# Down-projection: six sums of seven paired and woven matmul by matmul, with three weight forms moved to other tiles

## The chip, the cores and the metric

The kernel runs on one core of one Trainium2 chip. The metric is the device time of one execution in microseconds (us), the median of several runs. Below, PE is TensorE (matmuls), PEld its weight loads, DVE is VectorE, ACT is ScalarE, POOL is GpSimd, and SP is SyncE, which issues most DMAs. Inside the profiled execution, times are counted from the first instruction of the program.

## The reference, cut to what matters

```python
g = sigmoid((x * gate_w).sum(-1, keepdims=True))      # x: (2, 1, 4096, 640)
a = A_ref(x, w1, b1, w2, b2)      # real FFT, complex block MLP, soft threshold, inverse FFT
b = (gelu(x @ w_gate) * (x @ w_up)) @ w_down          # 640 -> 1728 -> 640
return g * a + (1 - g) * b
```

The change lies in the last product, the down-projection `h @ w_down`: 8192 tokens, 1728 rows of weights, 640 columns of output.

## The kernel before, in words

**Precision.** All operands are fp32 numbers split in two: a high part that ACT rounds (`high`, line 275) and a low part, the rest, that DVE subtracts (`low`, line 278). A product is three matmuls: high by high, low by high, high by low. `split` makes both parts.

**Order of the work.** First the gate and up projections (line 472, `run`, with 256 columns to a matmul), interleaved with the forward transform; then the spectral MLP; last, from about 1810 us on, the down-projection with the last stage of the inverse transform. This last stage is a loop of 32 steps over `c_seq` (batch and a pair of token groups of 128 tokens each).

**One step of the down-projection.** Two token groups are multiplied together by Winograd's scheme for 2 by 2 blocks: seven products instead of eight. Each product multiplies a combination of the hidden activations (`a11`, `s2`, `s3`, `s1`, `a12`, `a22`, `s4`) by a combination of the weights (`b11`, `t2`, `t3`, `t1`, `b21`, `t4`, `b22`, called forms). A product sums over seven chunks `j` of 128 rows into one PSUM bank: 21 matmuls of 128 by 128 by 320 columns, and 20 where the last chunk is half empty (the forms in `HALF`). That is 144 matmuls a step. In each, the activations are the stationary operand (`ho`) and the weights (`wx`) the moving one: for each `j`, high activations with high weights, low with high, high with low. In front of these, `inv2` (line 1161) does 12 matmuls of the inverse transform.

`down` (line 1188) does the seven products one after another, in the order of the list above, each followed by DVE or ACT work that reads the bank. Between two products stands a hook. The hooks call `step(k)` (line 1459), in which the operands of later products are made: `h_load` (DMA of four activation tiles for the next step), `h_s3`, `h_s2`, `h_s1` (sums on POOL), `h_s4` (on DVE), `h_op` (the split of one activation operand: two ACT and two or three DVE instructions), `c_load` and `c_split` (the inverse transform's data: two DMAs, then four splits), `v_load` (its matrix, issued by POOL), and `flush` (the stores that were put aside). Each engine executes its instructions in the order in which the code emits them; waits are made from the dependences.

**Tiles.** SBUF tiles come from tags with a fixed number of buffers: `big` (18 of 5120 bytes to a partition), `small` (18 of 2560), `tiny` (15 of 1024), `mid` (14 of 4096). The first three start at multiples of 128 bytes. Between them and `mid` lies a spacer of 112 words, 448 bytes, which is three and a half times 128, so each `mid` tile starts 64 bytes past a multiple of 128. Below, a tile or slice that starts at a multiple of 128 bytes is called plain and one that starts 64 bytes past it shifted. 1280 bytes, the width of one form's part, is ten times 128, so neighbouring parts in one tile are alike. In `c_split` (line 1105) the high parts start 16 words into a `mid` tile, which makes them plain, and the low parts 32 or 352 words, which leaves them shifted. A buffer that is reused waits for the last use of what it held; of the free ones, the one that has been free longest is taken. The weights stay in 14 `big`, 6 `small` and 10 `mid` tiles for the whole stage, so four `big` buffers are left for activation operands, and one operand takes one.

**Which part of a form lies where.** The parts are written to DRAM (`wdf`, `wdl`) by `wd_pre` in columns that `HI` and `LO` (lines 1011 and 1012) number, and read back by `wd_load`: columns 0 to 7 into two `big` tiles, 8 and 9 into a `small` one, 10 to 12 into a `mid` tile, and the one part in `wdl` into a `mid` tile for three `j`. So before the change the high parts of all seven forms, and the low parts of `b11`, `t2`, `t3`, are plain; the low parts of `t1` (from `wdl`), `b21`, `b22`, `t4` are shifted.

**The loads of the weights** are spread by hand over the last steps of the spectral MLP (the table `fin`, line 1412). Those of `S + 1`, the last, and of hook 0 of the first down step stand together in the SP queue.

Of the kernel before, what the change touches and what calls it, by code (L numbers as in the profile page):

```python
# [15 lines left out]
P = 128  # L16
# [197 lines left out]
def spectral_mix_kernel(ctx: ExitStack, tc: tile.TileContext, a):  # L214
# [793 lines left out]


    FORMS = ["b11", "t2", "t3", "t1", "b21", "t4", "b22"]  # L1010
    HI = {"b11": 0, "t2": 2, "b21": 4, "t3": 5, "t1": 6, "t4": 8, "b22": 9}
    LO = {"b11": 1, "t2": 3, "t3": 7, "b21": 10, "b22": 11, "t4": 12}

    def wd_pre(j):
        o = {}
        pair = (j, j + 6) if j < 6 else (12, 13)

        def loads():
            for t in pair:
                wd_raw(t)  # L1020

        def sums(k):
            def f():
                if not o:
                    r1, r2 = (RAW.pop(("d", t)) for t in pair)
                    o.update(b11=r1[:, :320], b12=r1[:, 320:], b21=r2[:, :320], b22=r2[:, 320:])
                n, p, q = (("t1", "b12", "b11"), ("t2", "b22", "t1"), ("t3", "b22", "b12"), ("t4", "b21", "t2"))[k]
                if k % 2 == 0:
                    o["x"] = small([P, 2, 320], name="wx")
                o[n] = o["x"][:, k % 2]  # L1030
                nc.vector.tensor_sub(o[n], o[p], o[q])
            return f

        def form(n):
            def f():
                w = small([P, 2, 320], F32R, name="wf")
                if j == 6 and n in HALF:
                    x = o[n][:64]
                    nc.gpsimd.memset(w[64:, 1].bitcast(F32), 0.0)
                    split(w[:64, 0], w[:64, 1], x)  # L1040
                    high(w[64:, 0], x)
                else:
                    split(w[:, 0], w[:, 1], o[n])
                if n == "t1":
                    st(dr(wdf[j], 320 * HI[n], [[13 * 320, P], [1, 320]]), w[:, 0].bitcast(F32))
                    st(dr(wdl, 320 * j, [[7 * 320, P], [1, 320]]), w[:, 1].bitcast(F32))
                else:
                    st(dr(wdf[j], 320 * HI[n], [[13 * 320, P], [320 * (LO[n] - HI[n]), 2], [1, 320]]), w.bitcast(F32))
# [11 lines left out]
    def wd_load(j, part):  # L1060
# [9 lines left out]
        if part < 2:  # L1070
            t = big([P, 4, 320], F32R, name="wx")
            go(t.rearrange("p h d -> p (h d)"), wdf[j], 13, 4 * part, 4)
            for k, (n, h) in enumerate((("b11", 0), ("b11", 1), ("t2", 0), ("t2", 1)) if part == 0 else
                                       (("b21", 0), ("t3", 0), ("t1", 0), ("t3", 1))):
                put(n, h, t[:, k])
        elif part == 2:
            if j < 6:
                t = small([P, 2, 320], F32R, name="wx")
                go(t.rearrange("p h d -> p (h d)"), wdf[j], 13, 8, 2)
                put("t4", 0, t[:, 0])  # L1080
# [3 lines left out]
            for k, n in ((0, "b21"), (352, "b22"), (672, "t4")):  # L1084
                put(n, 1, x[:, k:k + 320])
        else:
            x = mid([P, 1024], F32R, name="wx")
            n = 3 if j < 6 else 1
            go(x[:, :320 * n], wdl, 7, j, n)
            for k in range(n):  # L1090
                WM.setdefault(j + k, {}).setdefault("t1", [None, None])[1] = x[:, 320 * k:320 * k + 320]
            if j == 6:
                go(x[:, 336:976], wdf[6], 13, 8, 2)
                put("t4", 0, x[:, 336:656])
                put("b22", 0, x[:, 656:976])

    def c_load(i):
# [90 lines left out]
    def down(i, u, hooks):  # L1188
# [4 lines left out]
        c1, c2 = slice(0, 320), slice(320, 640)  # L1193
        acc = lambda: bank()[:, :320]

        def blk(a_, b_):
            h = HO.pop((i, a_))
            ops = []
            for j, (hh, hl) in enumerate(h):
                wh, wl = WM[j][b_]  # L1200
                ops += [(hh, wh), (hh, wl)] if j == 6 and a_ in HALF else [(hh, wh), (hl, wh), (hh, wl)]
            return ops
        hooks[0]()
        e = small([P, 2, 320], name="e")
        A = acc()
        run(A, blk("a11", "b11"))
        nc.scalar.activation(e[:, 0], A, AF.Copy)
        hooks[1]()
        B = acc()
        run(B, blk("s2", "t2"))  # L1210
        nc.vector.tensor_add(e[:, 0], B, e[:, 0])
        hooks[2]()
        C = acc()
        run(C, blk("s3", "t3"))
        nc.vector.tensor_add(e[:, 1], C, e[:, 0])
        hooks[3]()
        E = acc()
        run(E, blk("s1", "t1"))
        for x in (E, e[:, 1]):
            nc.vector.scalar_tensor_tensor(u2[:, c2], x, g2, u2[:, c2], op0=OP.mult, op1=OP.add)  # L1220
        hooks[4]()
        run(A, blk("a12", "b21"), first=False)
        nc.vector.scalar_tensor_tensor(u1[:, c1], A, g1, u1[:, c1], op0=OP.mult, op1=OP.add)
        hooks[5]()
        Dd = acc()
        run(Dd, blk("a22", "t4"))
        nc.vector.tensor_add(e[:, 1], Dd, e[:, 1])
        nc.vector.scalar_tensor_tensor(u2[:, c1], e[:, 1], g2, u2[:, c1], op0=OP.mult, op1=OP.add)
# [4 lines left out]
        nc.vector.scalar_tensor_tensor(u1[:, c2], e[:, 0], g1, u1[:, c2], op0=OP.mult, op1=OP.add)  # L1233
        st(out[b, n1], u1)

# [172 lines left out]
    def events(i, j):  # L1408
        for f, *args in todo.get((i, j), []):
# [11 lines left out]
           S - 2: [(h_load, 0, 0), *wl(1, 2), (h_load, 0, 1)],  # L1421
           S - 1: [(c_split, 0), (h_op, 0, "a11"), *wl(1, 3, 4, 5), *wl(0, 6), (h_s3, 0, nc.gpsimd), (c_load, 1)],
           S: [(h_s2, 0), (h_op, 0, "s2"), (c_split, 1)],
           S + 1: [*wl(1, 6), *wl(3, 0, 3, 6), (flush,), *wl(2, 6), (wd_later,), *wl(2, 4), (wd_later,), (h_s1, 0)]}
    for i in range(S + 2):
        events(i, 0)
        flush()
# [23 lines left out]
            f(*args)  # L1451


    for i in range(len(c_seq)):
        n = i + 1 if i + 1 < len(c_seq) else None
        if i:
# [2 lines left out]
        def step(k):  # L1459
            def f():  # L1460
# [28 lines left out]
        down(i, uu, [step(k) for k in range(7)])  # L1489
    flush()  # L1490


# [19 lines left out]
```

## Time and profile before

| | |
|---|---|
| median of 3 runs | 2545.61 us (2543.27 to 2547.45) |
| the profiled execution, its own time | 2545.72 us |
| its span, first to last instruction | 2544.0 us |
| granted TensorE clock, mean | 1.000 |
| PE, PEld busy | 2536.2, 2532.0 us |
| DVE busy | 2060.3 us (81%) |
| ACT, POOL busy | 1501.1, 376.2 us |
| matmuls of the down-projection (`wx` by `ho`) | 4608 |

A row of the costliest groups reads: line, engine, operation, tiles written and read, shapes, count, then busy time and mean duration in ns, then the engine's idle time ahead of them and what ended it. Rows of the timeline have the start and the length in us of a run of equal instructions, and their count. A run of n equal matmuls that follow each other without a wait lasts n - 1 intervals from start to start and one duration of a single matmul, which is about 0.31 us for 320 columns; so the interval can be worked out from one row.

### The profile page before, as it was taken

The page shows a single profiled execution, that of the slowest core. Times are in us where ns is not written, and L with a number is a line of the kernel's source. Part 1 is how long each engine was busy: PE and PEld are TensorE (multiplying, and loading weights), DVE is VectorE, ACT ScalarE, POOL GpSimd, SP SyncE. Part 2 cuts the span into 40 slices and gives each one's busy share as a digit, 9 for nine tenths or more (in the row PEclk, how much of TensorE's full clock was granted, in tenths as well). Part 3 has the DMA queues.
Part 4 walks back from the last instruction along what each step waited for, and adds up shares of the span by engine and source line. Part 5 has one row for each costly group of instructions (what it writes and reads, how often), then busy time and mean ns, then how long its engine had stood idle before and what let it go on. Part 6 is the DMA issues. An engine that isn't in the chain of part 4 may idle for free.

```text
span 2544.0 us, 54373 instructions
## 1 busy us (share of the span) xinstructions
PE 2536.2 (100%) x20317; PEld 2532.0 (100%) x20317; DVE 2060.3 (81%) x4214; ACT 1501.1 (59%) x3489; POOL 376.2 (15%) x379
## 2 busy tenths in 40 slices
PE   9999999999999999999999999999999999999999
PEld 9999999999999999999999999999999999999999
DVE  7778767777777766766667788888899999999998
ACT  5555555666665655555556788788644444445443
POOL 0000000000000000000003111111133333333332
PEclk9999999999999999999999999999999999999999
DMA  6565657676767677776667454548744444344442
GB/s 223 188 226 187 219 170 229 200 245 210 222 208 251 194 227 227 225 226 210 220 224 222 129 162 145 160 141 268 286 151 140 153 156 149 125 148 156 155 137 92
DMA packets 347212, 483.76 MB, mean 190 GB/s; under 512 B 24828, under 2 KB 223740, under 8 KB 346948
## 3 DMA queue, kind: packets, MB, share of 16 engines
q1 hardware_dynamic: 332116, 438.47, 54.2%
q0 software_dynamic: 14832, 41.82, 4.6%
q8 instruction: 160, 2.62, 0.4%
q14 instruction: 104, 0.85, 0.1%
HBM read 300.55 MB, written 179.64 MB: 189 GB/s over the span
## 4 chain that ended last, share of the span: by engine, by line
PE 97%; DVE 1%; DMA 1%; ACT 0%; issue 0%; POOL 0%; DVEq 0%; SPq 0%; POOLq 0%; ACTq 0%
PE bank L472 76%; PE bank L295 14%; PE bank L798 3%; PE bank L632 1%; PE bank L879 1%; PE bank L880 1%; DMA s<-scr 0%; PE bank L881 0%; PE bank L1272 0%; DMA scr<-is 0%; DMA wx<-wdf 0%; DVE ho L279 0%; DMA hraw<-hD 0%; DVE xo L279 0%; DVE xd L430 0%
## 5 line engine op out<-in xcount | busy, mean ns | idle before, releaser
L472 PE MATMUL bank<-xo,w 128*128 128x256 f32 x11736 | 1361.2, 277 | 0.3 <-ACT u L498 0.3
L472 PEld LDWEIGHTS bank<-xo,w 128*128 128x128 f32 x11736 | 1352.6, 188 | 0.8 <-ACT u L498 0.7
L472 PE MATMUL bank<-wx,ho 128*128 128x320 f32 x4608 | 677.1, 308 | 1.1 <-DVE ho L279 1.1
L472 PEld LDWEIGHTS bank<-wx,ho 128*128 128x128 f32 x4608 | 672.6, 188 | 1.9 <-DVE ho L279 1.9
L498 ACT ACTIVATE u<-bank 128x256 f32<-128x256 f32 x408 | 156.7, 384 | 257.0 <-PE bank L472 250.4
L279 DVE TENSOR_TENSOR ho<-hraw,ho 128x640 fp32r<-128x640 f32 (+3 forms) x384 | 279.6, 770 | 4.6 <-ACT ho L276 2.6
L276 ACT ACTIVATE ho<-hraw 128x640 fp32r<-128x640 f32 x320 | 166.5, 574 | 64.8 <-PE bank L472 49.8
L498 ACT ACTIVATE p<-bank 128x256 f32<-128x256 f32 x204 | 78.5, 385 | 150.2 <-PE bank L472 67.1
L279 DVE TENSOR_TENSOR xo<-xraw,xo 128x512 fp32r<-128x512 f32 x209 | 143.5, 687 | 24.7 <-ACT xo L276 24.2
L531 DVE TENSOR_TENSOR u<-bank,u 128x256 f32<-128x256 f32 x204 | 86.1, 422 | 89.7 <-ACT u L498 86.8
L279 DVE TENSOR_TENSOR xs<-xr,xs 64x640 fp32r<-64x640 f32 x128 | 105.0, 820 | 57.6 <-ACT xs L276 55.1
L1183 ACT ACTIVATE uu<-bank,gs 128x320 f32<-128x320 f32 x120 | 54.5, 527 | 158.0 <-PE bank L295 155.2
L295 PE MATMUL bank<-wm,h 128*128 128x320 f32 (+1 forms) x792 | 137.6, 309 | 0.0
L276 ACT ACTIVATE xo<-xraw 128x512 fp32r<-128x512 f32 x208 | 130.3, 627 | 7.2 <-DMA xraw<-in_xT_dram 5.4
L540 DVE TENSOR_TENSOR u<-bank,u 128x256 f32<-128x256 f32 x204 | 85.6, 420 | 60.4 <-PE bank L472 59.5
L634 DVE TENSOR_TENSOR as<-bank,as 64x320 f32<-64x320 f32 x256 | 113.8, 483 | 25.1 <-ACT as L633 24.0
L585 POOL MEMSET h<- 64x512 f32 x16 | 8.4, 522 | 749.9 <-PE bank L632 407.7
L295 PEld LDWEIGHTS bank<-wm,h 128*128 128x128 f32 (+1 forms) x792 | 117.9, 185 | 1.3
L276 ACT ACTIVATE ho<-hs 128x640 fp32r<-128x640 f32 (+1 forms) x128 | 71.9, 577 | 78.7 <-PE bank L472 60.2
L514 DVE TENSOR_TENSOR p<-bank,p 128x256 f32<-128x256 f32 x204 | 86.7, 425 | 37.1 <-PE bank L472 32.7
L279 DVE TENSOR_TENSOR s2s<-s,s2s 128x320 fp32r<-128x320 f32 x128 | 112.1, 933 | 1.6 <-ACT s2s L276 1.6
L633 ACT ACTIVATE as<-bank 64x320 f32<-64x320 f32 x256 | 96.8, 427 | 16.6 <-PE bank L632 14.1
(165 smaller groups left out, 3499.0 us busy)
## 6 DMA issues: line engine op xcount, KB each, us to landing
xo<-xD SPq DMA_DIRECT2D x124, 512.0 KB
xraw<-in_xT_dram SPq DMA_DIRECT2D x225, 256.0 KB
hD<-h SPq DMA_DIRECT2D x224, 256.0 KB
hraw<-hD SPq DMA_DIRECT2D x128, 320.0 KB
xD<-xo POOLq DMA_DIRECT2D x64, 512.0 KB, 4.4
sc<-scr SPq DMA_DIRECT2D x65, 320.0 KB
xr<-in_x_dram SPq DMA_DIRECT2D x64, 320.0 KB
scr<-as SPq DMA_DIRECT2D x64, 320.0 KB
```

The lines of the kernel that those rows point to most:

```text
L276: nc.scalar.activation(dst, src, AF.Copy, scale=scale)
L279: eng.tensor_sub(dst, src, hi.bitcast(F32))
L295: nc.tensor.matmul(dst, l, r, start=i == 0, stop=i == len(ops) - 1)
L472: nc.tensor.matmul(dst, l, r, start=first and i == 0, stop=i == len(ops) - 1, skip_group_check=True)
L498: copy = lambda d, s_: nc.scalar.activation(d, s_, AF.Copy)
L514: nc.vector.tensor_add(p1, A, p1)
L531: nc.vector.tensor_add(u4, C, u4)
L540: nc.vector.tensor_add(u2, C, u2)
L633: nc.scalar.activation(stg[hi, cs], pa[lo, :320], AF.Copy)
L634: nc.vector.tensor_add(stg[hi, cs], pa[hi, :320], stg[hi, cs])
L798: nc.tensor.matmul(pz[:, kp * P:(kp + 1) * P], SC[b, c, kp][:, o:o + P], ft, start=True, stop=True)
L1183: nc.scalar.activation(uu[n2][:, cs], pe[:, :320], AF.Copy, scale=gs[:, b, 0, n2:n2 + 1])
```

## The change

1. `HI` and `LO` are numbered anew. The high parts of `t1`, `b21`, `t4` go to columns 10 to 12, the `mid` tile (shifted), and their low parts to plain tiles. `b22` keeps a plain high part, and its low part takes the place in `wdl` that the low part of `t1` had (shifted). The two DMAs that filled the `mid` tile become one.
2. In `down`, from the second step on, six products are done in three pairs by the new function `duo`: (`a11 b11`, `a22 t4`), (`s2 t2`, `s1 t1`), (`s3 t3`, `a12 b21`). For each `j`, the six matmuls of a pair alternate between two banks; the moving parts are, in order: first form high, first form high, second form high, first form low, second form low, second form high. With the new places that is plain, plain, shifted, plain, plain, shifted. `s4 b22` stays by itself at the end. The first step (`i == 0`) keeps the old order, one product after another.
3. The hooks are moved to suit: inside a pair a hook stands ahead of `j == 4`, there is an eighth hook at the end, and operands, loads and POOL sums are made in another order.
4. In `fin[S + 1]` the loads from `wdl` (part 3) move behind `flush` and behind the part 2 loads of chunks 6 and 4.

```diff
-    HI = {"b11": 0, "t2": 2, "b21": 4, "t3": 5, "t1": 6, "t4": 8, "b22": 9}
-    LO = {"b11": 1, "t2": 3, "t3": 7, "b21": 10, "b22": 11, "t4": 12}
+    HI = {"b11": 0, "t2": 2, "t3": 4, "b22": 9, "t1": 10, "b21": 11, "t4": 12}
+    LO = {"b11": 1, "t2": 3, "t3": 5, "t1": 6, "b21": 7, "t4": 8}
...
-            later.append(lambda: (go(x[:, :320], wdf[j], 13, 10, 1), go(x[:, 352:992], wdf[j], 13, 11, 2)))
+            later.append(lambda: go(x[:, :960], wdf[j], 13, 10, 3))
...
+        def duo(X, x, Y, y, hook, more=False):
+            n = [0, 0]
+            hx, hy = rows(*x), rows(*y)
+            tot = [sum(map(len, h)) for h in (hx, hy)]
+            for j, (p, q) in enumerate(zip(hx, hy)):
+                if j == 4:
+                    hook()
+                for k, op in ((0, p[0]), (0, p[1]), (1, q[0]), (0, p[2]), (1, q[-1]), *([(1, q[1])] if len(q) == 3 else ())):
+                    nc.tensor.matmul((X, Y)[k], *op, start=n[k] == 0 and not (more and k), stop=n[k] == tot[k] - 1,
+                                     skip_group_check=True)
+                    n[k] += 1
...
+        if i:
+            Dd = acc()
+            duo(A, ("a11", "b11"), Dd, ("a22", "t4"), hooks[1])
+            nc.scalar.activation(e[:, 0], A, AF.Copy)
+            hooks[2]()
+            B, E = acc(), acc()
+            duo(B, ("s2", "t2"), E, ("s1", "t1"), hooks[3])
+            nc.vector.tensor_add(e[:, 0], B, e[:, 0])
+            scaled(u2[:, c2], E, g2)
+            hooks[4]()
+            C = acc()
+            duo(C, ("s3", "t3"), A, ("a12", "b21"), hooks[5], True)
+            nc.vector.tensor_add(e[:, 1], C, e[:, 0])
+            scaled(u2[:, c2], e[:, 1], g2)
+            scaled(u1[:, c1], A, g1)
...
-           S + 1: [*wl(1, 6), *wl(3, 0, 3, 6), (flush,), *wl(2, 6), (wd_later,), *wl(2, 4), (wd_later,), (h_s1, 0)]}
+           S + 1: [*wl(1, 6), (flush,), *wl(2, 6), (wd_later,), *wl(2, 4), (wd_later,), *wl(3, 0, 3, 6), (h_s1, 0)]}
...
+    SEQ = dict(enumerate(("s3", "s1", "a12", "a22", "s4")))
+    DUO = {0: "s1", 2: "s3", 3: "a12", 4: "s4"}
...
-                if k < 5:
-                    if k == 0:
-                        h_s4(i)
-                    h_op(i, ("s3", "s1", "a12", "a22", "s4")[k])
+                if k == (1 if i else 0):
+                    h_s4(i)
+                op = (SEQ if i == 0 else DUO).get(k)
+                if op:
+                    h_op(i, op)
                 if n is not None:
                     if k in (1, 2):
                         h_load(n, k - 1)
-                    if k == 2 and n > 1:
-                        c_load(n)
-                        v_load(n)
+                    if n > 1:
+                        if k == 0:
+                            c_load(n)
+                        if k == 3:
+                            v_load(n)
+                            c_split(n)
                     if k == 4:
                         h_s3(n, nc.gpsimd)
                         h_s2(n, nc.gpsimd)
                     if k == 5:
                         h_op(n, "a11")
-                        if n > 1:
-                            c_split(n)
                     if k == 6:
+                        h_op(n, "a22")
+                        h_s1(n, nc.gpsimd)
+                    if k == 7:
                         h_op(n, "s2")
-                        h_s1(n, nc.gpsimd)
```

More of the change, by code (lines that the diff above doesn't have):

```diff
@@ L1205, in down @@
         A = acc()
[L1206 to L1226, printed above, removed]
+        if i:
[13 more added lines that the diff above has]
+            scaled(u1[:, c1], A, g1)
+        else:
+            run(A, blk("a11", "b11"))
+            nc.scalar.activation(e[:, 0], A, AF.Copy)
+            hooks[1]()
+            B = acc()
+            run(B, blk("s2", "t2"))
+            nc.vector.tensor_add(e[:, 0], B, e[:, 0])
+            hooks[2]()
+            C = acc()
+            run(C, blk("s3", "t3"))
+            nc.vector.tensor_add(e[:, 1], C, e[:, 0])
+            hooks[3]()
+            E = acc()
+            run(E, blk("s1", "t1"))
+            for x in (E, e[:, 1]):
+                scaled(u2[:, c2], x, g2)
+            hooks[4]()
+            run(A, blk("a12", "b21"), first=False)
+            scaled(u1[:, c1], A, g1)
+            hooks[5]()
+            Dd = acc()
+            run(Dd, blk("a22", "t4"))
         nc.vector.tensor_add(e[:, 1], Dd, e[:, 1])
-        nc.vector.scalar_tensor_tensor(u2[:, c1], e[:, 1], g2, u2[:, c1], op0=OP.mult, op1=OP.add)
+        scaled(u2[:, c1], e[:, 1], g2)
         st(out[b, n2], u2)
```

43 lines of the change are left out of this document (25 added, 18 removed).

## The prediction

> **What bounds the kernel now.** I read the page's busy times and chain first, then the waits of the down stage, then the timeline of PE block by block.
>
> ```profile
> PE 2536.2 (100%) x20317; PEld 2532.0 (100%) x20317; DVE 2060.3 (81%) x4214; ACT 1501.1 (59%) x3489; POOL 376.2 (15%) x379
> ...
> PE 97%; DVE 1%; DMA 1%; ACT 0%; issue 0%; POOL 0%; DVEq 0%; SPq 0%; POOLq 0%; ACTq 0%
> ```
> ```profile
> 2245.88 20.97 PE bank L472 x144
> 2266.85 1.74 PE bank L295 x12
> 2268.60 20.97 PE bank L472 x144
> ```
>
> The chain of waits is PE from end to end, and in the down stage it is nothing but matmuls: 20.97 us for the 144 of a step and 1.74 for the 12 of the inverse transform, 22.71 us a step. A step gets shorter only if the matmuls follow each other faster. Whether they can is seen where one step is cut into its products:
>
> ```profile
> 2271.51 6.32 PE L472 MATMUL bank<-wx,ho 128*128 128x320 f32 x42
> ```
> ```profile
> 2277.66 6.10 PE L472 MATMUL bank<-wx,ho 128*128 128x320 f32 x41
> ```
> ```profile
> 2283.60 5.97 PE L472 MATMUL bank<-wx,ho 128*128 128x320 f32 x40
> ```
>
> These are `t2` and `t3`, then `t1` and `b21`, then `t4` and `b22` of one step. With 0.31 us off for the last matmul, the interval is 6.01/41 = 146.6 ns, then 5.79/40 = 144.8, then 5.66/39 = 145.1. Same shape, same clock (1.000), no wait. What differs is where the weights lie: in the first row all are plain, in the other two every third matmul (the low part) is shifted. In the gate and up projections all moving tiles are shifted and the weights loaded plain:
>
> ```profile
> 599.82 9.91 PE L472 MATMUL bank<-xo,w 128*128 128x256 f32 x86
> ```
>
> Its interval is (9.91 - 0.28)/85 = 113.3 ns for 256 columns; 146.6 scaled to 256 columns would be 117.3. So a shifted moving operand against plain stationary ones is cheaper, and a step has 28 of them (7 each in `t1`, `b21`, `t4`, `b22`). 144 matmuls at 146.6 would be 21.11 us; the chain has 20.97, so the 28 save 0.14 us, 5.0 ns each. Within `t1` and `b21` it is 41 x 1.8 / 14 = 5.3. How much one can save at most is bounded by the durations of this group (minimum, median, maximum in ns): the shortest are 7 below the median.
>
> ```profile
> L472 PE MATMUL bank<-wx,ho x4608: 302/309/412, 1810.5 to 2539.1; 128*128 128x320 f32 x192
> ```
>
> TensorE: Matmul & The Clock Gate, section Back-to-back issue gap, in the Trainium skill has the gap depend on the columns alone, N/2.4 + 2.5 ns warm, which is an estimate of 135.8 ns for 320. The trace has 146.6 and 144.8 for equal N, so the rule misses the very thing that is changed here; what follows if it held is the fourth rival.
>
> **The change part by part. 1. The rhythm of the matmuls.** After it, `t1` has 14 shifted matmuls (two use the high part), `t4` and `b21` 13 each, `b22` 7: 47 in place of 28. Woven, they come as plain, plain, shifted all through a pair, the order that `t1` and `b21` have now; it breaks only at the last chunk of two pairs and at the end of `b22`. At 5.0 ns each, 47 save 0.235 us, 0.095 more than now; at 7, 0.33, 0.19 more. Nothing in the trace shows two open banks alternating; a change of bank from one product to the next costs nothing that can be seen (42 matmuls over `t2` and `t3` keep 146.6). Bounds: from 0 saved (all 144 at 146.6: +0.14) to -0.19. I take 6.0 ns, between the two, because long unbroken runs show more than short ones (5.3 over 41, less over the broken 40): 0.282, **-0.14 us a step. Over 31 steps -4.3 us.**
>
> **2. The first step** keeps the old order, so `t1`, `t4`, `b21` become shifted, shifted, plain. The nearest row is in the spectral MLP: there the stationary tiles are shifted, two matmuls of three stream plain data and the third shifted data, which seen from the stationary operand is the same order.
>
> ```profile
> 1782.14 1.04 PE L295 MATMUL bank<-wm,h 128*128 128x320 f32 x6
> ```
>
> 0.73/5 = 146 ns: no saving. So the first step loses about 0.1 us of its 0.14; ends 0 and +0.14. **+0.1.**
>
> **3. DVE work.** No instruction is added; the same splits, sums and evacuations are done. But DVE is nearly full.
>
> ```profile
> 2223.17:2245.88 22.71, 22.71 (x158) 22.71 (x158) 22.41 (x39) 11.01 (x24) 8.54 (x7) 1.00 0.45 151
> 2245.88:2268.60 22.72, 22.72 (x159) 22.72 (x158) 21.92 (x37) 11.00 (x24) 8.17 (x7) 1.00 0.46 148
> ```
> ```profile
> L279 DVE TENSOR_TENSOR ho<-hraw,ho 128x128 fp32r<-128x128 f32 x44 | 33.7, 767 | 0.0
> ...
> L279 DVE TENSOR_TENSOR ho<-hs,ho 128x640 fp32r<-128x640 f32 x44 | 35.9, 815 | 0.0
> ...
> L1220 DVE SCALAR_TENSOR_TENSOR uu<-e,gs,uu 128x320 f32<-128x320 f32 x22 | 15.3, 695 | 0.8
> ...
> L1223 DVE SCALAR_TENSOR_TENSOR uu<-bank,gs,uu 128x320 f32<-128x320 f32 x22 | 12.1, 551 | 2.6 <-PE bank L472 2.2
> ...
> L1211 DVE TENSOR_TENSOR e<-bank,e 128x320 f32<-128x320 f32 x22 | 10.8, 491 | 6.5 <-PE bank L472 6.5
> ...
> L279 DVE TENSOR_TENSOR ho<-hs,ho 64x128 fp32r<-64x128 f32 x22 | 6.3, 285 | 0.7
> L279 DVE TENSOR_TENSOR ho<-hs,ho 128x128 fp32r<-128x128 f32 x22 | 6.2, 280 | 0.0
> ```
> ```profile
> L1139 POOL TENSOR_TENSOR hraw<-hs,hraw 128x640 f32<-128x640 f32 x22 | 35.8, 1626 | 70.2 <-DVE ho L279 70.2
> L1139 POOL TENSOR_TENSOR hraw<-hs,hraw 128x256 f32<-128x256 f32 x22 | 21.7, 985 | 0.0
> ```
>
> The busy columns are PE, PEld, DVE, ACT, POOL: DVE 21.9 to 22.4 of 22.7 us. Part of that is waiting beside POOL: the same 128x128 subtraction takes 280 ns where POOL is idle and 767 where it is not. The tightest new deadline is `a22`: its low part is now due at the head of a step, in the first pair, and its split is queued on DVE behind five evacuations of the third pair. Those last 0.49 + 0.70 + 0.55 + 0.49 + 0.55 = 2.8 us and the split 0.82 + 0.28 + 0.29 = 1.4, together 4.2 us from 0.3 us after the third pair. PE meanwhile does `s4 b22` (2.9 us), the inverse transform (1.74) and five matmuls of the new pair (0.7): 5.3 us. **Margin 0.9 us, no wait taken.** If all of `h_s1` on POOL (1.63 + 0.99 = 2.6 us) blocked DVE just there, PE would wait 1.7 us a step, the upper end. Three of the five evacuations read a bank and one SBUF tile; such a one (491 ns) shows no mark of POOL. Behind `a22` stand the evacuation of `s4 b22` and the splits of `s2` and `s1`, due 6 us later in the second pair. Operands `s3`, `a12`, `s4` wait for one of the four `big` buffers, which now come free two at a time at the end of a pair; each is due a whole pair later (6 us against 1.2 to 1.4 us of split). SBUF — State Buffer, section Who interferes with whom, in the Trainium skill says that DVE with two SBUF inputs and a POOL instruction that reads SBUF exclude each other; the 767 against 280 agrees.
>
> **4. Loads at the start of the stage.** Here a cover goes. SP's queue around the first step:
>
> ```profile
> 1809.21 3.47 SPq L1066 DMA_DIRECT2D wx<-wdl  x3
> 1813.16 0.76 SPq L1066 DMA_DIRECT2D wx<-wdf  x1
> 1816.18 1.49 SPq L256 DMA_DIRECT2D scr<-is  x2
> 1817.78 4.95 SPq L1066 DMA_DIRECT2D wx<-wdf  x8
> ```
> ```profile
> 1822.41 5.23 DMA wx<-wdf
> ```
> ```profile
> 1816.00:1818.00 2.00, 2.00 (x16) 2.00 (x15) 2.00 (x5) 1.74 (x5) 0.00 (x0) 1.00 1.01 402
> ...
> 1822.00:1824.00 2.00, 2.00 (x16) 2.00 (x15) 1.83 (x4) 2.00 (x6) 0.00 (x0) 1.00 0.98 344
> ```
>
> The DMA engines are full (share 0.98 to 1.01), so what lands last is set by the bytes ahead of it. The last of the eight loads, the `mid` tile of chunk 5, lands at 1822.41 + 5.23 = 1827.64. The four loads in rows one and two move behind the store that SP waits for at 1816.2, still ahead of chunk 5; the bytes ahead of chunk 5 stay the same, so it lands at about 1827.6 again. Before, that tile held low parts needed from `b21` on. Now it holds the high part of `t1`:
>
> ```profile
> 1822.46 3.22 PE L472 MATMUL bank<-wx,ho 128*128 128x320 f32 x21
> ```
>
> `t1` starts at 1822.46 and reaches chunk 5 after 15 matmuls, at 1824.66. PE then waits 3.0 us, once. Bounds: 0 (the queue drains early) to 4. Against it, PE's waits for the second step's operands, which do not hang on PE, are overtaken:
>
> ```profile
> 1819.43 21.51 PE L472 MATMUL bank<-wx,ho 128*128 128x320 f32 x144 [0.76 <-DVE ho L279]
> 1841.27 1.00 PE L472 MATMUL bank<-wx,ho 128*128 128x320 f32 x5 [0.33 <-DVE ho L279]
> ```
>
> 144 intervals at 145.6 would end 0.4 us sooner, and the next start is 0.5 us late: 0.8 us, all of which goes. **+3.0 - 0.8 = +2.2 us.** One DMA in place of two for each `mid` tile costs nothing beside a full queue.
>
> **Sum.** -4.3 + 0.1 + 2.2 = -2.0 us on the profiled execution's 2545.72 (span 2544.0 and 1.7 around it), which is 0.1 over the median of the runs: **2543.7 us.**
>
> **The rivals.** *First, full pay and no wait at the start*: 7 ns each (-0.19 x 31 = -5.9), chunk 5 lands in time (0), the 0.8 us goes: 2545.72 - 5.9 + 0.1 - 0.8 = 2539.1. For it: the queue has one DMA less to issue per chunk; against it: full engines. *Second, slower: the woven order doesn't pay.* In the pairs the second shifted matmul follows two different low parts, and two banks alternate; the trace shows neither. If pairs run at 146.6, only `b22` saves: 0.14 x 21/28 = 0.105 us a step lost over 32, +3.4, and +2.2: 2551.3. It decides from the point where the interval in a pair exceeds 144.8. *Third, slower: DVE late for `a22`.* Once POOL holds DVE for more than the 0.9 us of margin, PE waits at the head of each step; 0.3 us of it would add 9.3: 2553.0. For it: DVE is 97% busy and POOL blocks it; against it: POOL's two earlier sums fall into the time in which DVE waits for a pair's end. *Fourth, the new places change nothing in the rhythm*: the step stays at 22.71 us, and the start costs 2.2: 2547.9. That is also what the Trainium skill's rule on the gap would give (TensorE: Matmul & The Clock Gate, Back-to-back issue gap); rows one and two of the blocks speak against it.
>
> **How the numbers follow.** A change under 0.2%, 5.1 us, is about what a measurement of this kernel cannot tell from none. Forecast 0.52 (2541.5 to 2546), first rival 0.18, second 0.12, third 0.12, fourth 0.06. Faster by over 0.2% (under 2540.6): the first, 0.18. Same: forecast and fourth, 0.58. Slower: second and third, 0.24. The range runs from the first rival to just under the third: 2539.1 to 2552.5.
>
> **What would show it.** A step's 144 matmuls in the chain at 20.83 us and 22.57 with the inverse transform; a pair of 41 or 42 at 144.5 ns or less; PE's waits in the stage once, about 3 us, for `wx` near 1824.7. Wrong would be: PE idle at the head of each step with DVE `ho` as releaser (third), pairs at 146.6 (second), or no wait near 1824 (first).

## The result, and the profile after

| | before | after |
|---|---|---|
| median of the runs | 2543.7 us (2542.52 to 2547.45, 22 runs) | 2549.28 us (2547.13 to 2551.13, 22 runs) |
| ratio, 95% interval | | 1.0019 (1.0012 to 1.0026) |
| the profiled execution, its span | 2545.72, 2544.0 us | 2548.73, 2547.0 us |
| granted clock, mean | 1.000 | 0.998 |
| from the first `wx` matmul to the end of the span | 2544.0 - 1810.46 = 733.5 us | 2547.0 - 1809.89 = 737.1 us |

By the ratio of the runs the change makes the kernel slower by 0.19%, 4.8 us (the two medians differ by 5.6), where 2 us less was forecast. The last row of the table leaves out the stages ahead, whose end moves by some us from run to run (1809.3 to 1813.6 in the traces below): within the stage it is +3.6 us.

The page's busy times and the shares of the chain, of after:

```profile
PE 2533.7 (99%) x20317; PEld 2529.6 (99%) x20317; DVE 2053.1 (81%) x4214; ACT 1491.7 (59%) x3489; POOL 372.4 (15%) x379
...
PE 98%; DMA 1%; DVE 1%; ACT 0%; issue 0%; SPq 0%; DVEq 0%; ACTq 0%
```

PE is busy for 2.5 us less than before, and yet the span is 3.0 us longer: PE now stands still for several us. The chain of waits of after, at the same place as in the prediction (start, length, what), shows where it got faster; L1218 is the matmul in `duo`, L472 the one in `run`:

```profile
2250.81 17.92 PE bank L1218 x124
2268.73 2.90 PE bank L472 x20
2271.63 1.75 PE bank L295 x12
```

17.92 + 2.90 = 20.82 us for the 144 matmuls of a step instead of 20.97; 20.81 where the first piece is 17.91. That is 0.15 to 0.16 us a step, 4.7 us over 31 steps. The loss must be elsewhere. PE's waits from 1700 us on (line, releaser: total, times, longest; the line left out, here and below, is a wait of L295 in the stage ahead, under 1 us):

```profile
PE bank L472 <- DMA wx<-wdf: 6.6, 2, 4.9
...
```

PE waits for weights twice, 6.6 us in all; before it never did. The timeline of PE in the first step, with the idle time ahead of a run in brackets:

```profile
1809.89 6.32 PE L472 MATMUL bank<-wx,ho 128*128 128x320 f32 x42
...
1817.79 5.04 PE L472 MATMUL bank<-wx,ho 128*128 128x320 f32 x33
1824.49 0.70 PE L472 MATMUL bank<-wx,ho 128*128 128x320 f32 x3 [1.66 <-DMA wx<-wdf]
1830.13 12.45 PE L472 MATMUL bank<-wx,ho 128*128 128x320 f32 x66 [4.93 <-DMA wx<-wdf]
```

After `t3` and twelve matmuls of `t1` PE waits 1.66 us for the `mid` tile of chunk 4, does three matmuls, and waits 4.93 us for that of chunk 5. Then the last row: 66 matmuls at 146.5 ns would be 65 x 0.1465 + 0.31 = 9.8 us, and they take 12.45. Why the loads are late is in SP's timeline of after:

```profile
1804.19 1.26 SPq L256 DMA_DIRECT2D scr<-is  x2
1806.17 0.33 SPq L1068 DMA_DIRECT2D wx<-wdf  x1
1814.62 1.21 SPq L256 DMA_DIRECT2D scr<-is  x2
1815.87 1.84 SPq L1068 DMA_DIRECT2D wx<-wdf  x3
1817.77 2.24 SPq L1068 DMA_DIRECT2D wx<-wdl  x3
1820.06 2.79 SPq L1068 DMA_DIRECT2D wx<-wdf  x3
```

From 1806.5 to 1814.62 SP issues nothing: it stands at the `flush`, whose stores wait for the copies into `is`. The load at 1806.17 is all that it issues between the two pairs of stores. In before there was one such load, too, and behind it the four that were moved (1809.21 to 1813.9). The window from 1814 to 1816 us, first in before, then in after with some of those that follow (busy us of PE, PEld, DVE, ACT, POOL, then granted clock, DMA share, GB/s):

```profile
1814.00:1816.00 2.00, 2.00 (x15) 2.00 (x15) 1.81 (x5) 2.00 (x6) 0.00 (x0) 1.00 1.02 419
```
```profile
1814.00:1816.00 2.00, 2.00 (x16) 2.00 (x15) 2.00 (x6) 1.74 (x5) 0.00 (x0) 1.00 0.18 65
...
1824.00:1826.00 2.00, 0.70 (x3) 0.44 (x3) 0.47 (x2) 0.00 (x0) 0.00 (x0) 0.91 1.04 410
1826.00:1828.00 2.00, 0.00 (x0) 0.00 (x0) 0.00 (x0) 0.00 (x0) 0.00 (x0) 0.50 1.03 414
...
1832.00:1834.00 2.00, 2.00 (x9) 2.00 (x8) 1.86 (x3) 0.42 (x1) 1.90 (x2) 0.50 0.40 138
1834.00:1836.00 2.00, 2.00 (x9) 2.00 (x9) 2.00 (x3) 0.00 (x0) 2.00 (x2) 0.53 0.04 11
1836.00:1838.00 2.00, 2.00 (x16) 2.00 (x15) 1.94 (x3) 1.05 (x2) 1.44 (x2) 1.00 0.00 0
```

The DMA engines ran dry: a share of 0.18 at 65 GB/s where before had 1.02 at 419. The load of chunk 5 in the chain of after:

```profile
1822.53 7.46 DMA wx<-wdf
```

It lands at 1829.99, 20.1 us after the stage's start; in before it was 1827.64 - 1810.46 = 17.2. And while PE waits, the clock falls to 0.50, at about 1825.6 (the window with 0.91), and stays there until about 1835.9 (the window with 0.53): 9 matmuls in 2 us instead of 14 to 16. The long wait had begun only half a us before the fall, at 1825.19; the wait of 1.66 us and three matmuls lie just ahead of it. So the trace of after gives: 6.6 us of wait, 12.45 - 9.8 = 2.6 us of slow clock, the two waits of before (0.76 and 0.33) gone, the rhythm -4.7: 6.6 + 2.6 - 1.1 - 4.7 = +3.4, of +3.6.

### The profile page after: what moved, and what is told of

Same layout as the page of the kernel before. It is cut to its first block, busy times and chain, and to the rows that moved or that the text cites. A ratio compares the mean times of both kernels' runs of the same rounds, so it can differ in the third digit from the quotient of the medians.

```text
span 2547.0 us, 54577 instructions
## 1 busy us (share of the span) xinstructions
PE 2533.7 (99%) x20317; PEld 2529.6 (99%) x20317; DVE 2053.1 (81%) x4214; ACT 1491.7 (59%) x3489; POOL 372.4 (15%) x379
## 4 chain that ended last, share of the span: by engine, by line
PE 98%; DMA 1%; DVE 1%; ACT 0%; issue 0%; SPq 0%; DVEq 0%; ACTq 0%
PE bank L472 56%; PE bank L1218 22%; PE bank L295 14%; PE bank L798 3%; PE bank L632 1%; PE bank L879 1%; PE bank L880 1%; DMA wx<-wdf 1%; DMA s<-scr 0%; PE bank L881 0%; PE bank L1310 0%; DVE xd L430 0%; DVE xo L279 0%; DVE h L543 0%; DVE w L279 0%
## 5 line engine op out<-in xcount | busy, mean ns | idle before, releaser
L472 PE MATMUL bank<-xo,w 128*128 128x256 f32 x11736 | 1360.4, 277 | 0.3 <-ACT u L498 0.3
L472 PEld LDWEIGHTS bank<-xo,w 128*128 128x128 f32 x11736 | 1351.8, 188 | 0.8 <-ACT u L498 0.7
L1218 PE MATMUL bank<-wx,ho 128*128 128x320 f32 x3844 | 560.8, 306 | 0.0
L1218 PEld LDWEIGHTS bank<-wx,ho 128*128 128x128 f32 x3844 | 557.2, 188 | 0.0
L279 DVE TENSOR_TENSOR ho<-hraw,ho 128x640 fp32r<-128x640 f32 (+3 forms) x384 | 272.1, 749 | 22.6 <-ACT ho L276 19.7
L295 PE MATMUL bank<-wm,h 128*128 128x320 f32 (+1 forms) x792 | 137.6, 309 | 0.0
L472 PE MATMUL bank<-wx,ho 128*128 128x320 f32 x764 | 119.5, 312 | 6.6 <-DMA wx<-wdf 6.6
L472 PEld LDWEIGHTS bank<-wx,ho 128*128 128x128 f32 x764 | 114.7, 192 | 7.1 <-issue 5.2
L295 PEld LDWEIGHTS bank<-wm,h 128*128 128x128 f32 (+1 forms) x792 | 117.9, 185 | 1.3
```

Source lines behind the costliest of these rows:

```text
L279: eng.tensor_sub(dst, src, hi.bitcast(F32))
L295: nc.tensor.matmul(dst, l, r, start=i == 0, stop=i == len(ops) - 1)
L472: nc.tensor.matmul(dst, l, r, start=first and i == 0, stop=i == len(ops) - 1, skip_group_check=True)
L1218: nc.tensor.matmul((X, Y)[k], *op, start=n[k] == 0 and not (more and k), stop=n[k] == tot[k] - 1, skip_group_check=True)
```

## The experiments

My theory: the weave pays what was forecast, and the order of the loads takes more than that back, by the wait and by the clock. The rivals: the loss is in the weave or in the new places (two banks, another order on DVE); and, for the reason of the gain, that each shifted tile saves a fixed time against that the order of plain and shifted tiles decides.

| run | what it is | median, us | ratio to before (95%) | 144 matmuls, us |
|---|---|---|---|---|
| old_load_order | after, loads as before | 2545.02 | 1.0001 (0.9992 to 1.001) | 20.81 |
| early_loads | after, loads ahead of the stores | 2540.05 | 0.9983 (0.9974 to 0.9992) | 20.81 |
| weave_alone | old places, old loads, woven | 2544.2 | 0.9994 (0.9985 to 1.0003) | 20.94 |
| places_alone | new places, not woven | 2546.25 | 1.0004 (0.9995 to 1.0013) | 21.01 |
| filled_wait | after, matmuls in the wait | 2546.96 | 1.001 (1.0001 to 1.0019) | 20.81 |
| neighbours | early_loads, other order in a pair | 2547.49 | 1.001 (1.0 to 1.0019) | 20.94 to 21.22 |
| all_shifted | early_loads, shifted tiles alone | 2547.95, one run | | 21.12 |
| spacer_128 | before, plain tiles alone | 2620.72, one run | | 21.10 |
| alternate | early_loads, plain and shifted in turn | 2544.6, one run | | 20.97 |
| low_parts_last | early_loads, `b22`'s low parts last | 2540.87 | 0.9987 (0.9978 to 0.9996) | 20.81 |
| flush_first | early_loads, stores sooner | 2540.64 | 0.9985 (0.9976 to 0.9994) | 20.81 |
| order_alone | before, loads of early_loads | 2548.98 | 1.0019 (1.001 to 1.0027) | 20.97 |

The runs stand in three groups that shared a chip and the runs of before: the first four (before 2545.27), the next four in the table (2545.14), and the last four (2544.36).

### The loads: old_load_order and early_loads

The row `S + 1` of the table `fin`, as in before, put into after:

```diff
-           S + 1: [*wl(1, 6), (flush,), *wl(2, 6), (wd_later,), *wl(2, 4), (wd_later,), *wl(3, 0, 3, 6), (h_s1, 0)]}
+           S + 1: [*wl(1, 6), *wl(3, 0, 3, 6), (flush,), *wl(2, 6), (wd_later,), *wl(2, 4), (wd_later,), (h_s1, 0)]}
```

> The changed kernel with the old line of loads for the last step of the MLP (wdl ahead of the stores); nothing else is undone. Theory (the DMA engines ran dry because the wdl loads were moved behind the stores): chunk 5 lands about 2.3 us earlier, PE waits 3 us for it and not at all for chunk 4, the clock stays up: 2541 to 2543. Rival (the bytes ahead of chunk 5 alone decide, and they are the same): the waits stay at 6 to 7 us and the time at 2548 to 2550.

And in early_loads with everything that PE needs first ahead of the stores, chunk 5 too, which leaves hook 0 of the first step:

```diff
-           S + 1: [*wl(1, 6), (flush,), *wl(2, 6), (wd_later,), *wl(2, 4), (wd_later,), *wl(3, 0, 3, 6), (h_s1, 0)]}
+           S + 1: [*wl(1, 6), *wl(2, 6), (wd_later,), *wl(2, 4), (wd_later,), *wl(2, 5), (wd_later,), (flush,), *wl(3, 0, 3, 6), (h_s1, 0)]}
...
-                if (i, k) == (0, 0):
-                    wd_load(5, 2)
-                    wd_later()
```

> The changed kernel with its weight loads in another order: the mid tiles of chunks 6, 4 and 5 are loaded ahead of the stores that SP waits for, and those from wdl behind them. Theory (the loads): the change's rhythm saves 0.15 us in each of 31 steps, 4.7 us, and what it loses is PE's wait for the mid tiles of chunks 4 and 5 in the first step (6.6 us) with the clock at 0.50 after it; then this kernel shows no PE wait for wx and runs at 2538 to 2539.5, 4 to 6 us under the kernel before (2543.7). Rival (the first step's operands or the moved hooks cost the time, not the loads): PE waits elsewhere instead and the time stays at 2546 or more.

PE's waits in the stage, first in old_load_order, then in early_loads:

```profile
PE bank L472 <- DMA wx<-wdf: 2.6, 2, 1.4
PE bank L1218 <- DVE ho L279: 0.9, 1, 0.9
...
```
```profile
PE bank L1218 <- DVE ho L279: 1.2, 1, 1.2
...
```

With the old order the weights are waited for 2.6 us instead of 6.6 and the clock stays at 1.00; with the early order they are not waited for at all. What is left is a wait for the low part of `a22` at the head of the second step, 0.9 and 1.2 us. One thing went against what was expected of old_load_order: the 2.6 us are not one wait for chunk 5 but 1.20 us for chunk 4 and 1.37 for chunk 5. The first `wx` matmuls of the stage, first in old_load_order, then in early_loads:

```profile
1811.37 6.32 PE L472 MATMUL bank<-wx,ho 128*128 128x320 f32 x42
```
```profile
1813.59 6.32 PE L472 MATMUL bank<-wx,ho 128*128 128x320 f32 x42
```

From there to the end of the span the stage takes 2543.2 - 1811.37 = 731.8 and 2542.2 - 1813.59 = 728.6 us, 1.7 and 4.9 less than before; the timed ratios lie 0.0018 and 0.0036 under that of after. The times do not confirm the 1.7 us of old_load_order: its median of 2545.02 us can't be told from before, and 2541 to 2543 was expected. So the order of the loads alone decides between 0.17% gained (early_loads), nothing that the timing can tell (the old order) and 0.19% lost (the change). Woven steps in early_loads:

```profile
1860.54 17.91 PE bank L1218 x124
1878.45 2.90 PE bank L472 x20
```

### The halves: weave_alone and places_alone

weave_alone is after with the `HI`, `LO`, `form`, `wd_load` and the row `S + 1` of before: it weaves, and the tiles lie as they did. places_alone is before with the new `HI`, `LO`, `form` and `wd_load` and the loads of early_loads: 47 shifted tiles a step, one product after another. The heart of the first:

```diff
-    HI = {"b11": 0, "t2": 2, "t3": 4, "b22": 9, "t1": 10, "b21": 11, "t4": 12}
-    LO = {"b11": 1, "t2": 3, "t3": 5, "t1": 6, "b21": 7, "t4": 8}
+    HI = {"b11": 0, "t2": 2, "b21": 4, "t3": 5, "t1": 6, "t4": 8, "b22": 9}
+    LO = {"b11": 1, "t2": 3, "t3": 7, "b21": 10, "b22": 11, "t4": 12}
```

> The changed kernel with the old places of the parts and the old loads: the pairs are woven into two banks, but only one matmul in six is shifted (the low part of the second form). Theory (places and their rhythm pay, not the banks): a step's 144 take 20.93 to 21.05 us, about as before, 2542 to 2546. Rival (alternating banks is what pays): 20.82 us as in the changed kernel, 2538 to 2540.

> The kernel before, its seven sums one after another, with only the new places of the parts (and the loads of the first run here, so that nothing waits at the start). In t1, t4, b21 the order is then shifted, shifted, plain. Theory (the rhythm plain, plain, shifted is what pays): the three sums run at 146.6 ns a matmul, only b22 saves, a step's 144 take 21.05 to 21.1 us, 0.1 more than before: 2546 to 2547.5. Rival (every shifted matmul saves by itself, 47 of them): 20.8 us a step, 2538 to 2540, and the weaving is for nothing.

One step in the chain, first weave_alone, then places_alone:

```profile
2245.07 18.04 PE bank L1216 x124
2263.12 2.90 PE bank L472 x20
```
```profile
2246.80 21.01 PE bank L472 x144
```

The weave alone gives 20.94 us, the places alone 21.01 (21.05 to 21.1 was expected), before has 20.97, both together 20.81. Neither half is worth anything that the timing can tell. So a shifted tile doesn't save a fixed time: places_alone has the same 47 as after and is the slowest of the four. It is the order that counts, and the two banks are not needed for it: in one bank, `t1` and `b21` of before had 144.8 ns as plain, plain, shifted. weave_alone goes through its pairs as plain five times and then shifted, places_alone as shifted, shifted, plain, after as plain, plain, shifted.

### What in the order: neighbours, all_shifted, alternate, spacer_128

In neighbours two shifted tiles of a chunk stand side by side:

```diff
-                for k, op in ((0, p[0]), (0, p[1]), (1, q[0]), (0, p[2]), (1, q[-1]), *([(1, q[1])] if len(q) == 3 else ())):
+                for k, op in ((0, p[0]), (0, p[1]), (1, q[0]), *([(1, q[1])] if len(q) == 3 else ()), (0, p[2]), (1, q[-1])):
```

> The kernel with early loads (run early_loads), but within each chunk of a pair the order is plain, plain, shifted, shifted, plain, plain in place of plain, plain, shifted twice: the same 47 shifted matmuls in a step, in half as many runs. Theory one (each shifted moving tile saves its 6 ns wherever it stands, as the prediction summed it): a step's 144 matmuls stay at 20.81 us, the ratio to before stays at 0.998. Theory two (what counts is how often a shifted tile follows two plain ones; a second shifted one adds little, as the blocks with shifted, shifted, plain at 145.6 ns in places_alone suggest): half of the saving goes, 20.96 us a step, 4.6 us more over 31 steps, ratio 1.000.

```profile
2246.36 18.19 PE bank L1218 x124
...
2269.20 18.04 PE bank L1218 x124
...
2291.88 18.32 PE bank L1218 x124
```

These are three steps in a row of its chain; with 2.90 for the rest they take 21.09, 20.94 and 21.22 us. The second theory is right for the shortest steps (20.94 against 20.96 expected; 14 of the 30 in the chain), and the others lose more than it allowed; the mean is 21.03. Why equal steps differ here stays open. The timed ratio, 0.0027 over that of early_loads, agrees.

The other three change which moving tiles are plain and which shifted. all_shifted and alternate do it by reading the same one or two tiles of a chunk again and again in place of those of the seven forms; whether that by itself matters is not tested. Their edits:

```diff
-                wh, wl = WM[j][b_]
+                wh, wl = WM[j][b_] if i == 0 else 2 * (WM[j]["t1"][0],)
```
```diff
-                    nc.tensor.matmul((X, Y)[k], *op, start=n[k] == 0 and not (more and k), stop=n[k] == tot[k] - 1,
+                    w = WM[j][("b11", "t1")[sum(n) % 2]][0]
+                    nc.tensor.matmul((X, Y)[k], op[0], w, start=n[k] == 0 and not (more and k), stop=n[k] == tot[k] - 1,
```

> The kernel with early loads, but from the second step on every moving operand is the high part of t1 of its chunk, which is shifted: 144 of 144 moving tiles are shifted. It computes six of the seven products with wrong weights; the loads, the counts of matmuls and all other work stay. Only the interval of the matmuls is read. Theory one (each shifted tile saves 6 ns): 21.11 - 144 x 0.0064 = 20.19 us for the 144 of a step, 140 ns each, as the gate projection has 113.3 at 256 columns with all moving tiles shifted. Theory two (only a change from plain to shifted saves): no gain at all, 146.6 ns, 21.11 us a step.

> The kernel with early loads, but from the second step on the moving operands are the high part of b11 (plain) and that of t1 (shifted) of the chunk in turn: plain, shifted, plain, shifted. It computes the products with wrong weights; loads, counts and all other work stay. Theory one (what saves is each passage from plain to shifted, about 6.4 ns, as runs of one shifted tile, of two and of all 144 suggest so far): 72 passages a step, 21.11 - 72 x 0.0064 = 20.65 us. Theory two (a passage saves only where two plain tiles stand ahead of it): little or no saving, 21.0 to 21.1 us. Theory three (each shifted tile beside a plain one saves by itself): also 20.65, so one and three are not told apart here; the runs with two shifted tiles in a row do that.

The chain of all_shifted, then of alternate:

```profile
2268.87 18.19 PE bank L1218 x124
2287.06 2.93 PE bank L472 x20
```
```profile
2267.43 18.06 PE bank L1222 x124
2285.49 2.91 PE bank L472 x20
```

144 shifted tiles give 21.12 us, which is no gain at all, and 72 in turn with plain ones 20.97, a gain of some 2 ns for each passage instead of 6. In spacer_128 the `mid` tiles start at multiples of 128 bytes:

```diff
-            gap.extend([tiny([P, 1], name="gap"), pool.tile([P, 112], F32, name="gap", tag="gap", bufs=1)])
+            gap.extend([tiny([P, 1], name="gap"), pool.tile([P, 128], F32, name="gap", tag="gap", bufs=1)])
```

> The kernel before with the spacer ahead of the mid tiles 128 words long in place of 112, so that mid tiles start at multiples of 128 bytes, as all others. Nothing else is changed, the output is the same. Theory one (64 bytes between moving and stationary tile save about 6 ns a matmul): the down step is 21.11 us for 144, 146.6 ns each, instead of 20.97, and in the gate and up projections, whose moving tiles are all in mid tiles, the interval goes from 113.3 to about 119 to 120 ns; with some 11736 matmuls there that is 65 to 80 us on the whole. Theory two (the intervals differ for another reason: the number of columns, the tags, the reuse of an operand): 113.3 ns and 20.97 us stay.

Its chain in the down stage, a run of the gate and up projections in its timeline, and a run of as many in before:

```profile
2250.77 21.10 PE bank L472 x144
```
```profile
600.18 11.80 PE L472 MATMUL bank<-xo,w 128*128 128x256 f32 x97
```
```profile
598.55 11.18 PE L472 MATMUL bank<-xo,w 128*128 128x256 f32 x97
```

21.10 us with (nearly) all tiles plain: the base from which the prediction counted, 21.11, is confirmed. At 256 columns the interval is (11.80 - 0.28)/96 = 120.0 ns with plain moving tiles and (11.18 - 0.28)/96 = 113.5 with shifted ones. The busy time of all these matmuls, in spacer_128 and in before:

```profile
L472 PE MATMUL bank<-xo,w 128*128 128x256 f32 x11736 | 1430.7, 283 | 0.0
```
```profile
L472 PE MATMUL bank<-xo,w 128*128 128x256 f32 x11736 | 1361.2, 277 | 0.3 <-ACT u L498 0.3
```

That is 69.5 us more, and with 32 x 0.13 = 4 us in the down stage nearly all of the 74.9 us by which the span grows (2618.9 against 2544.0). So at 256 columns a run of shifted tiles alone saves 6.5 ns a matmul, and at 320 it saves nothing. There the orders with at least two plain tiles ahead of each shifted one save some 6 ns for each: 0.29 us for 47 in early_loads, 21.10 - 20.94 = 0.16 us for 28 in weave_alone. Why the two widths differ these runs don't settle.

### The clock: filled_wait

```diff
-            run(E, blk("s1", "t1"))
+            X, ops = acc(), blk("s1", "t1")
+            for n, (l, r) in enumerate(ops):
+                for m in range({12: 11, 15: 32}.get(n, 0)):
+                    nc.tensor.matmul(X, *ops[0], start=True, stop=True, skip_group_check=True)
+                nc.tensor.matmul(E, l, r, start=n == 0, stop=n == len(ops) - 1, skip_group_check=True)
```

> The kernel after, with 43 extra matmuls of 320 columns in the first step, into a bank that nobody reads: 11 ahead of the wait for the mid tile of chunk 4 in t1, 32 ahead of that of chunk 5. They take 43 x 0.146 = 6.3 us, just under the 6.6 us that PE waits there now, so the loads, the waits' ends and the output are the same; only PE isn't idle. Theory one (the loss at the start is the wait, and on top of it the clock that drops to 0.50 because PE is idle): the granted clock stays at 1.00, the last 66 matmuls of t1 to b22 take 9.8 us instead of 12.45, and the run is 2.6 us shorter than the kernel after: about 2546.7, a ratio of 1.0009 to before. Theory two (the clock drops for a reason that has nothing to do with the idle PE, say the load of the DMA engines and PE together): the clock is 0.50 again for some 10 us, and the ratio stays at 1.0019 or gets worse.

Its timeline of PE (L1258 are the extra matmuls) and one of its windows:

```profile
1809.29 6.31 PE L472 MATMUL bank<-wx,ho 128*128 128x320 f32 x42
...
1824.75 4.85 PE L1258 MATMUL bank<-wx,ho 128*128 128x320 f32 x32
1830.84 1.11 PE L1259 MATMUL bank<-wx,ho 128*128 128x320 f32 x6 [1.23 <-DMA wx<-wdf]
1831.79 8.88 PE L472 MATMUL bank<-wx,ho 128*128 128x320 f32 x60
```
```profile
1832.00:1834.00 2.00, 2.00 (x16) 2.00 (x15) 1.97 (x3) 0.63 (x2) 1.18 (x1) 1.00 0.46 156
```

The wait for chunk 5 is filled but for 1.23 us, the clock is 1.00 in every window, and the 66 matmuls take 0.95 + 8.88 = 9.8 us instead of 12.45. So the slow clock comes from PE standing idle and costs 2.6 us; the rows show that directly. The time shows it less sharply: the ratio falls by 0.0009, as theory one expected, but the two intervals overlap. In these two traces only 736.7 against 737.1 us of the stage are left of it, since in this execution chunk 5 is reached 21.55 us after the stage's start (1830.84 - 1809.29) instead of 20.24 (1830.13 - 1809.89), and the second step waits 0.9 us for DVE, which the slow clock had hidden.

### Can it be better still: low_parts_last, flush_first, order_alone

low_parts_last takes the loads of part 3 out of the row `S + 1` of early_loads and puts them behind the next step's activations; flush_first sets `flush` ahead of chunk 5; order_alone is before with nothing but the loads of early_loads.

```diff
+                if (i, k) == (0, 3):
+                    for j in (6, 0, 3):
+                        wd_load(j, 3)
```

> The kernel with early loads, but the four loads of part 3 (the low parts of b22) stand in hook 3 of the first step, behind the eight loads of the next step's activations, in place of ahead of them. Those land about 3 us sooner, and the 1.2 us that PE waits at the head of the second step in early_loads goes; b22's low parts land near 1832 in that run's time, 1 to 2 us before they are needed. Theory one (the queue's order alone sets these waits): no PE wait above 0.5 us from the stage's start to the end of the second step, 1.2 us less than early_loads, ratio 0.9978. Theory two (the wait only changes its name, to wx from wdl in the last two products of the first step): the same sum of waits, ratio 0.998 to 0.999.

> The kernel with early loads, but with the flush ahead of the two loads of chunk 5 in place of behind them. SP waits at the flush for the second pair of copies, at about 1818.5, and no load of chunk 5 is issued before it. Theory one (a dry DMA queue is what delays the loads): some 15 engine-microseconds of queue remain at the flush, so nothing runs dry, chunk 5 lands within 1 us of the place it had, and the ratio stays at 0.998 to 0.999. Theory two (any load behind the flush lands late): PE waits 2 us or more for chunk 5's mid tile, ratio 0.9995 or more.

> The kernel before with nothing but the early order of the loads in the last row of the table: chunk 5 ahead of the flush, part 3 behind it. Theory one (early_loads gains by the rhythm, the order of the loads only keeps that gain): before had no wait for weights, so nothing is gained, ratio 0.9995 to 1.0005, and the 144 of a step stay at 20.97 us. Theory two (the order of the loads gains by itself, by activations or stores that land sooner): ratio 0.999 or less.

PE's waits, in this order:

```profile
PE bank L472 <- DMA wx<-wdf: 1.1, 1, 1.1
PE bank L472 <- DMA wx<-wdl: 0.5, 1, 0.5
```
```profile
PE bank L472 <- DVE ho L279: 0.8, 1, 0.8
...
PE bank L1218 <- DVE ho L279: 0.2, 1, 0.2
```
```profile
PE bank L472 <- DMA wx<-wdl: 3.8, 1, 3.8
```

In low_parts_last the wait at the second step is gone, and 1.6 us for the four loads that were put back have come in the last two products of the first step: theory two, the wait changed its name. flush_first behaves as its theory one says. The three good versions (0.9983, 0.9985, 0.9987) can't be told apart.

order_alone went against what I wrote: 0.19% slower. In the old places `wdl` holds the low parts of `t1`, the fourth product, not of `b22`, the last; moved behind the stores they land at 1825.6, and PE waits 3.8 us. The clock drops here too, in these windows of order_alone:

```profile
1824.00:1826.00 2.00, 0.40 (x1) 0.40 (x2) 0.91 (x3) 0.00 (x0) 0.00 (x0) 0.90 1.03 405
1826.00:1828.00 2.00, 2.00 (x9) 2.00 (x9) 0.00 (x0) 0.00 (x0) 0.00 (x0) 0.50 1.07 389
1828.00:1830.00 2.00, 2.00 (x12) 2.00 (x11) 0.00 (x0) 0.66 (x1) 0.03 (x1) 0.75 1.04 361
```

So moving part 3 back was right for the new places and would have been wrong for the old; what the change missed is to put something else in front of the stores.

## Why the prediction was wrong

**Step 1, the rhythm: right in size, half right in its reason.** 20.83 us a step was forecast, 20.81 came, -4.7 us over 31 steps instead of -4.3; the woven pairs do pay. But the sum was made as a price of 6 ns for each shifted tile, and the bound of 7 came from the same picture. places_alone, neighbours and all_shifted refute it: with 47, 47 and 144 shifted tiles they save 0.09, 0.16 at best and nothing. It came out because after keeps the very order (plain, plain, shifted) in which the 5.3 ns had been measured; that 0.29/47 = 6.2 ns came so near to the 6 chosen between 5.0 and 7 is in part luck. The row at 256 columns, used to say that a shifted tile is cheaper by itself, holds for 256 columns only. The formula of the Trainium skill (TensorE: Matmul & The Clock Gate, Back-to-back issue gap), given there for an isolated gap, has the columns alone and knows no such difference; equal widths gave 144.5 to 146.7 ns here.

**Step 2, the first step in the order shifted, shifted, plain: right within its bounds.** In places_alone this order costs 0.04 us a step over before; +0.1 was forecast, between 0 and +0.14.

**Step 3, DVE and `a22`: right.** From the second step on the trace of after has no PE wait in this stage; the margin of 0.9 us held. At the head of the second step that is owed to PE coming late: where the loads are mended, `a22` is waited for there, once, 0.9 us in old_load_order and 1.2 in early_loads.

**Step 4, the loads: this failed.** The words were "the bytes ahead of chunk 5 stay the same, so it lands at about 1827.6 again". The bytes did stay the same: from the stage's start to that landing the DMA engines moved 383 GB/s over 17.18 us in before, 335 over 20.10 in after, 6.6 and 6.7 MB. The time in which they could move them did not. But for one load that stayed, the four that left their place were the only work that SP had issued for the stretch in which it waits for the copies into `is`. The share of the engines, which the step quoted as full at 1816 and 1822, would have had to be asked for at 1814, with these four loads taken away. Chunk 5 came 2.9 us later, and chunk 4, which the step did not look at, was waited for as well: 6.6 us instead of 3.0. The second fault is the price of the wait. A wait of 3.0 us was added as 3.0; the two that came cost 2.6 us more by the clock. The 0.8 us that should vanish did, 1.1 even, but only behind waits as long as these. With the old order of the loads, in which the assumption holds, old_load_order waited 2.6 us for weights and its stage was 1.7 us shorter in the trace than that of before, near the -2.0 of the forecast; the timed runs (ratio 1.0001, 0.9992 to 1.001) show no gain.

The rivals for a slower result put the loss into the weave or on DVE; neither happened. A dry queue was in none of them. That 2549.28 still lies below the 2552.5 at the top of the range is luck: the range reached so high for these two.

## What to carry to other kernels

Before a DMA is moved behind an instruction on which its queue waits, count what is left in the queue for that wait: full DMA engines are a state of this order of issues, not a property of the stage. A wait of PE is not worth its length alone; look whether the granted clock follows it, and if it can't be avoided, matmuls into a spare bank keep the clock up (what they gained in time could not be told from noise here). Where an interval of matmuls depends on where tiles lie, measure the sequence that you mean to use, at its width, and don't price one tile of it.

## What the runs showed of the hardware that was not expected

- The clock fell to 0.50 at about 1825.6 both in after and in order_alone (windows of 0.91 and 0.90). In order_alone PE had stood idle for 3.8 us by then. In after the wait of 4.93 us was only 0.5 us old, with the wait of 1.66 us and 0.70 us of matmuls ahead of it. The clock stayed at 1.00 through waits of 1.20 and 1.37 us with 0.70 us of matmuls between them (old_load_order). When matmuls went on at 1830.13 in after it took until about 1835.9, 5.8 us, to come back, in order_alone about 3.4 (from 1825.60 to the middle of the window with 0.75). TensorE: Matmul & The Clock Gate, section What's actually happening, in the Trainium skill says that an idle window of about 3.4 us halves the clock and a busy one restores it; order_alone agrees in both, but in after PE had worked for 1.3 of the 3.4 us ahead of the fall, and 5.8 us is more than one window.
- At 320 columns the mean interval was 146.5 ns with 142 of 144 moving tiles plain, 146.7 with all shifted by 64 bytes, 145.6 in turn, and 144.5 as plain, plain, shifted; at 256 columns 120.0 plain and 113.5 shifted. No row explains it.
